# A decode block on one core: the last 5 KB of each row of one K tile loaded by transfers of 112, 3, 3, 3, 3, 2, 1 and 1 rows

## The chip, the core and the metric

The kernel runs on one core of one Trainium2 chip. The metric is the device time of one execution in microseconds (us); the time before is the median of three runs, 354.95 us (354.88 to 355.61). The profile is of one further execution, which took 354.43 us.

## The reference, cut to what matters

One token passes through an attention block with a long cache and a small feed-forward block. There are 32 query heads and 8 groups of K and V ("kv heads"); each group has 32768 cached positions of 128 values in bf16, which is 8 MB of K and 8 MB of V.

```python
mod = (silu(c) @ w_mod)                      # sa, ca, ga, sb, cb, gb
h = layernorm(x) * (1 + ca) + sa
q = h @ wq                                   # 32 heads of 128
scores = einsum('bhqd,bhkd->bhqk', q, k) * Dh ** -0.5   # k: 8 groups, 32768 positions
p = softmax(scores)
o = einsum('bhqk,bhkd->bhqd', p, v)
x = x + ga * (o @ wo)
h = layernorm(x) * (1 + cb) + sb
x = x + gb * (relu(h @ w1) @ w2)
```

With one token there is little arithmetic for each byte: nearly all of the work is to bring 8 groups of K and V, and the weights, into the core's memory once.

## The kernel before

**Tiles.** K and V of one group are loaded as one tile each, `Ksb{g}` and `Vsb{g}`, of 128 partitions (rows) by 256 positions by 128 values: 64 KB in each row. In the code a tile counts as four steps `u` of 64 positions (`TK = 64`, `NTILE = 4`). All large tiles live in one pool, `ring`, with three buffers (line 77), so the tile that is loaded next must wait until the tile three places before it has been read to the end. `wmq_sb` (the weights of the modulation and of Q) is the first of them and `tail_sb` (the weights `wo`, `w1`, `w2`) the last.

**The stream.** The list `stream` (lines 148 to 155) names every large load in order: `k0` (first half), `w_mod`, `wq`, `k0` (second half), then `k(g+1)` and `v(g)` in turns, from group 5 on in halves, at the end `wo` in four pieces, `w1` in two and `w2` in six. `need(key)` (line 158) loads along this list until the key asked for is there. `load` (line 108) makes the tile and its source, and calls `stream_dma` (line 140), which issues one DMA from the SP queue and keeps the order of the list. All these loads thus stand in one queue, and SP issues each as soon as its buffer is free. Nothing else but the 1 KB output is issued from SP; the two loads of `c` and `x` (1 KB in 8 rows each, line 169) are issued from ACT.

**The work on a tile.** For K: `turn_k` (line 416) transposes an eighth of the tile with DVE, in place (line 426), and `scores` multiplies it on PE (line 445) into `S_ps`. Then `softmax` works with PE, DVE and ACT. For V: `pv` (line 499) multiplies the probabilities by V on PE (line 507), in a loop for groups 0 to 4. In the main loop (line 630) the scores of group g+1 are worked out ahead of `pv` of group g. A K buffer comes free when its scores are done, a V buffer when its `pv` is.

**Loading order around the change.** Group 3's K, `Ksb3`, goes into the buffer that `Vsb0` held. It comes behind `Ksb2` and `Vsb1` in the queue, and ahead of `Vsb2` and `Ksb4`. `turn_k(3, u, half)` reads positions 64u + 32·half to 64u + 32·half + 31 of each row.

**Counting landings.** Each DMA is given one of eight completion counters, in turn. An instruction that needs a tile waits for the counters of the DMAs that wrote it. A DMA whose counter was used by an earlier DMA that nobody has waited for yet makes SP wait for that earlier one first.

**The end.** After the last piece of `w2` has landed, 16 small matmuls (line 767), two operations of DVE (lines 772 and 774) and the 1 KB output follow.

Of the kernel before, what the change touches and what calls it, by code (L numbers as in the profile page):

```python
# [17 lines left out]
def kernel(  # L18
# [15 lines left out]
    P = 128  # L34
# [8 lines left out]
    TK = 64  # L43
    NTILE = Sk // (P * TK)
# [8 lines left out]
    W1P = [(0, KT - 1), (KT - 1, KT)]  # L53

    OUT0, OUT1 = 30, 34
    assert Dh == 128 and REP == 4 and D == 512 and FT == W2P[-1][1] and NTILE == 4
    scale = float(Dh) ** -0.5
    eps = 1e-5
# [8 lines left out]
    def wo_v(i):  # L67
        g0, n = WOP[i]
        return A_wo[g0 * REP * Dh:(g0 + n) * REP * Dh, :].rearrange("(p r) d -> p r d", p=P)
# [32 lines left out]
    def piece(name, at, n):  # L102

        if name not in pieces:
            pieces[name] = ring.tile([P, NTILE * TK * Dh], BF16, tag="slot", name=name)
        return pieces[name][:, at:at + n]

    def load(key):
        kind = key[0]
        if kind == "wm":  # L110
            t = piece("wmq_sb", 0, WM).rearrange("p (kt n) -> p kt n", kt=KT)
            src = wm_v
        elif kind == "wq":
            t = piece("wmq_sb", WM, WQ).rearrange("p (kt n) -> p kt n", kt=KT)
            src = wq_v
        elif kind in "kv":
            g, steps = key[1], key[2]
            src = (kv if kind == "k" else vv)[g, :, TK * steps[0]:TK * (steps[-1] + 1), :]
            name = f"Ksb{g}" if kind == "k" else f"Vsb{g}"
            t = piece(name, TK * Dh * steps[0], TK * Dh * len(steps)).rearrange("p (j d) -> p j d", d=Dh)  # L120
        elif kind == "wo":
            g0, n = WOP[key[1]]
            t = piece("tail_sb", g0 * REP * D, n * REP * D).rearrange("p (r d) -> p r d", d=D)
            src = wo_v(key[1])
        elif kind == "w1":
            k0, k1 = W1P[key[1]]
            t = piece("tail_sb", WO + k0 * Dff, (k1 - k0) * Dff).rearrange("p (kt f) -> p kt f", f=Dff)
            src = w1_v[:, k0:k1]
        else:
            f0, f1 = W2P[key[1]]  # L130
            t = piece("tail_sb", WO + KT * Dff + f0 * D, (f1 - f0) * D).rearrange("p (f d) -> p f d", d=D)
            src = w2_v[:, f0:f1]
        stream_dma(t, src)
        if kind in "kv":
            for i, u in enumerate(steps):
                loaded[(kind, g, u)] = t[:, TK * i:TK * (i + 1), :]
        else:
            loaded[key] = t

    def stream_dma(dst, src):  # L140
        i = nc.sync.dma_start(out=dst, in_=src)  # L141
        tc.stamp_issue_order_token(i.ins, "sp_stream")
        if last_loop:

            tc.add_manual_dep(i.ins, last_loop[0], mybir.DependencyInfo(
                mybir.DependencyClass.NoSync, mybir.DependencyReason.DATA))

    whole, halves = [(0, 1, 2, 3)], [(0, 1), (2, 3)]
# [9 lines left out]
    def need(key):  # L158
        while key not in loaded:
            load(stream[pos[0]])  # L160
            pos[0] += 1
        return loaded[key]
# [19 lines left out]
    for hp in range(4):  # L182
        h, par = hp // 2, hp % 2
        src = AP(ib.tensor, ib.offset + 64 * h + par, [[ib.ap[0][0], P], [0, 4], [2, 32]])
# [130 lines left out]
    for u in range(2):  # L315
        for half in range(2):
            t = need(("k", 0, u))[:, 32 * half:32 * half + 32, :].rearrange("p j d -> p (j d)").bitcast(F32)
# [488 lines left out]
```

## Time and profile before

| what | value |
|---|---|
| runs before | 354.88, 354.95, 355.61 us |
| profiled execution: its time, its span | 354.43 us, 352.5 us |
| DMA traffic | 149.58 MB, mean 424 GB/s over the span |
| issues of K and of V (8 MB tiles, and pieces of them) | 11 and 12 |
| PE busy, DVE busy | 276.4 us (78%), 200.9 us (57%) |
| a transposition of an eighth of K on DVE | 2275 ns, 64 of them |

The span runs from the first to the last instruction; 1.9 us of the profiled execution lie around it. There are 16 DMA engines, and each large transfer is cut into packets, one for each row: 128 packets, 8 on each engine, with one packet of 4 bytes on each engine behind them that counts the landing up. A transfer's data have landed when all the engines that carry it have counted. The trace keeps start, duration and size of every packet but not the number of its engine.

### The profile page before, as it was taken

What the parts mean: (1) busy time and instruction counts of PE and PEld (TensorE: products, weight loads), DVE (VectorE), ACT (ScalarE), POOL (GpSimd) and SP (SyncE); (2) the same over time, 40 slices, a digit from 0 to 9 for tenths busy, and PEclk for the clock granted to TensorE, in tenths of its full rate; (3) what the DMA queues carried; (4) which work ended last, traced back from release to release, by engine and by line L of the source; (5) the groups of instructions that cost most, each with busy time, mean ns of one, the idle gap of its engine ahead of it and who ended that gap; (6) DMA issues with size and microseconds to landing.
All of it is one profiled execution on the core that took longest, in us unless ns stands there. A gap on an engine that the chain in (4) does not pass through costs nothing. (4 is left out here: it accounts for less than half of the span.)

```text
span 352.5 us, 3650 instructions
## 1 busy us (share of the span) xinstructions
PE 276.4 (78%) x1285; PEld 112.7 (32%) x1285; DVE 200.9 (57%) x226; ACT 25.1 (7%) x69; POOL 3.1 (1%) x15
## 2 busy tenths in 40 slices
PE   0055891995998599976998499867999789989976
PEld 0021330341333233422433233322444334434433
DVE  6662464984079613974099506975684357744142
ACT  1200103002000200001000200011000100011000
POOL 2000000000000000000000000000000000000000
PEclk9996897698999969996999989996999999999986
DMA  8999989989999999899899899999999999999995
GB/s 353 404 436 440 496 372 469 461 379 469 431 409 455 424 424 461 387 448 469 387 454 469 387 455 461 396 402 450 435 422 424 450 429 420 433 454 403 429 413 217
DMA packets 5379, 149.58 MB, mean 424 GB/s; under 512 B 632, under 2 KB 888, under 8 KB 1784
## 3 DMA queue, kind: packets, MB, share of 16 engines
q1 hardware_dynamic: 5336, 149.43, 98.5%
q8 instruction: 8, 0.13, 0.1%
q14 instruction: 3, 0.02, 0.0%
q10 hardware_dynamic: 32, 0.00, 0.0%
HBM read 149.42 MB, written 0.00 MB: 424 GB/s over the span
## 5 line engine op out<-in xcount | busy, mean ns | idle before, releaser
L426 DVE STREAM_TRANSPOSE Ksb<-Ksb 128x2048 f32<-128x2048 f32 x60 | 133.1, 2275 | 59.6 <-DMA Ksb<-in_A_k_cache_dram 59.6
L507 PE MATMUL o_ps<-Vsb,P_g 128*16 (+1 forms) x512 | 126.6, 405 | 13.3 <-ACT P_g L482 10.0
L445 PE MATMUL S_ps<-Ksb,qbd 128*128 128x512 bf16 x512 | 120.8, 388 | 10.4 <-DVE Ksb L426 8.7
L445 PEld LDWEIGHTS <-qbd 128*128 128x128 bf16 x512 | 49.8, 99 | 77.7 <-issue 21.8
L507 PEld LDWEIGHTS o_ps<-Vsb,P_g 128*16 x352 | 33.6, 95 | 68.2 <-issue 38.3
L507 PEld LDWEIGHTS <-P_g 128*16 128x16 bf16 x160 | 13.8, 90 | 19.0 <-issue 0.4
L407 ACT COPY qbd<-qrep_sb 32x16 bf16<-32x16 bf16 x32 | 6.4, 201 | 175.2 <-PE S_ps L445 174.0
L487 DVE STREAM_TRANSPOSE P_g<-P_g 128x1024 bf16<-128x1024 bf16 x8 | 10.0, 1245 | 14.1 <-ACT P_g L482 14.1
L458 DVE TENSOR_REDUCE m_p<-S_ps 128x1 f32<-128x1024 f32 x7 | 8.6, 1223 | 12.7 <-PE S_ps L445 12.7
L309 PE MATMUL mod_ps<-wmq_sb,siluT 128*1 128x512 bf16 x24 | 3.6, 623 | 9.9 <-DMA wmq_sb<-in_w_mod_dram 9.9
L318 DVE STREAM_TRANSPOSE Ksb<-Ksb 128x2048 f32<-128x2048 f32 x4 | 8.9, 2280 | 1.7 <-DMA Ksb<-in_A_k_cache_dram 1.7
L463 PE MATMUL mT_ps<-ident_f,m_p 128*1 128x128 f32 x8 | 2.2, 270 | 8.9 <-DVE m_p L458 7.9
L482 ACT ACTIVATE P_g<-S_ps,nbias 128x1024 bf16<-128x1024 f32 x8 | 8.9, 1114 | 0.2
L493 PE MATMUL L_ps<-Lexp,ones_f 128*128 128x4 f32 x16 | 3.1, 263 | 6.4 <-DVE Lexp L490 4.3
L496 DVE RECIPROCAL Linv<-L_ps 128x4 f32<-128x4 f32 x8 | 1.3, 164 | 11.7 <-PE L_ps L493 11.7
L479 ACT ACTIVATE nbias<-Mb_ps 128x1 f32<-128x1 f32 x8 | 1.4, 171 | 88.1 <-PE Mb_ps L477 88.1
L542 PE MATMUL acc_ps<-mask_sb,Y 16*128 16x4 f32 x16 | 3.1, 258 | 5.5 <-DVE Y L538 5.5
L239 PE MATMUL xc_ps<-cx_sel,wmq_sb 16*128 16x2 bf16 x4 | 0.3, 172 | 8.8 <-DVE wmq_sb L233 8.8
L535 DVE TENSOR_TENSOR o_ps<-o_ps,smask 16x512 f32<-16x512 f32 x8 | 5.3, 668 | 2.8 <-PE o_ps L507 2.8
L573 DVE CAST o_sb<-o_ps 128x4 bf16<-128x4 f32 (+2 forms) x4 | 0.7, 166 | 9.9 <-PE o_ps L569 9.9
L493 PEld LDWEIGHTS L_ps<-Lexp,ones_f 128*128 128x128 f32 x16 | 2.6, 203 | 9.7 <-issue 6.4
L538 DVE TENSOR_REDUCE Y<-o_ps 16x128 f32<-16x512 f32 x8 | 5.4, 679 | 0.3
(116 smaller groups left out, 80.6 us busy)
## 6 DMA issues: line engine op xcount, KB each, us to landing
Ksb<-in_A_k_cache_dram SPq DMA_DIRECT2D x6, 4096.0 KB, 30.3
Vsb<-in_A_v_cache_dram SPq DMA_DIRECT2D x5, 4096.0 KB, 29.5
wmq_sb<-in_A_wq_dram SPq DMA_DIRECT2D x1, 4096.0 KB, 28.1
Vsb<-in_A_v_cache_dram SPq DMA_DIRECT2D x2, 2048.0 KB, 35.5
wmq_sb<-in_w_mod_dram SPq DMA_DIRECT2D x1, 3072.0 KB, 18.9
tail_sb<-in_A_wo_dram SPq DMA_DIRECT2D x1, 2048.0 KB, 22.7
tail_sb<-in_B_w_dram SPq DMA_DIRECT2D x1, 1344.0 KB
tail_sb<-in_A_wo_dram SPq DMA_DIRECT2D x1, 1024.0 KB, 24.8
```

The source lines that it names most:

```text
L309: nc.tensor.matmul(dst[j // 4][32 * (j % 4):32 * (j % 4) + 1, :], lhsT=src_T[:, kt:kt + 1], rhs=w[:, kt, j * 512:(j + 1) * 512], start=(kt ...
L318: nc.vector.transpose(out=t, in_=t)
L407: nc.scalar.copy(out=o, in_=i)
L426: t = nc.vector.transpose(out=KTt.bitcast(F32), in_=KTt.bitcast(F32))
L445: nc.tensor.matmul(S_ps_tiles[g], lhsT=qbd[g % 2][:, hp, 4 * (7 - s):4 * (7 - s) + P], rhs=KTv[:, 16 * sl:16 * sl + 16, h, :, par], start= ...
L458: behind_loop(nc.vector.reduce_max(out=m_p[:], in_=S_g.rearrange("p g f -> p (g f)"), axis=AX.X))
L482: nc.scalar.activation(out=P_g[:], in_=S_g.rearrange("p g f -> p (g f)"), func=ACT.Exp, bias=nbias[:], scale=scale, accum_out=l_g[:],)
L487: behind_loop(nc.vector.transpose(out=P_g[:], in_=P_g[:]))
L493: nc.tensor.matmul(L_ps[:], lhsT=ones_f[:], rhs=Lexp[:], start=True, stop=True)
L507: nc.tensor.matmul(o_tiles[g][:], lhsT=PT, rhs=Vx, start=False, stop=False, skip_group_check=True)
L535: nc.vector.tensor_tensor(out=o, in0=o, in1=smask[:].unsqueeze(2).to_broadcast([16, 4, Dh]), op=ALU.mult,)
L538: nc.vector.tensor_reduce(out=Y[:], in_=o.rearrange("p s d -> p d s"), op=ALU.add, axis=AX.X)
```

## The change

Only the load of `Ksb3` is different. Its 256 positions are cut at position `EDGE` = 4·64 − 20 = 236. The first 236 positions of all 128 rows come by one transfer (59 KB in each row). The last 20 positions (5120 B in each row) come by eight: rows 0 to 111 by one, and rows 112 to 127 by seven of 3, 3, 3, 3, 2, 1 and 1 rows. The order in the queue is: the 112 rows, the first 3 rows, the 128 rows of 59 KB, then the other six. The bytes in all, and what is computed, are as before.

```diff
+    UNEVEN, FEW = 3, [(112, 115), (115, 118), (118, 121), (121, 124), (124, 126), (126, 127), (127, 128)]
+    EDGE = NTILE * TK - 20
...
-        stream_dma(t, src)
+        if key[:2] == ("k", UNEVEN):
+            whole = slice(0, EDGE)
+            last = [(slice(a, b), slice(EDGE, None)) for a, b in [(0, FEW[0][0])] + FEW]
+            for part in last[0:2] + [(slice(0, P), whole)] + last[2:]:
+                stream_dma(t[part], src[part])
+        else:
+            stream_dma(t, src)
```

The order of the instructions shows these waits on SP's queue, beside those of before: the transfer of 2 rows waits for `Ksb2` to have landed, the first of 1 row for `Vsb1`, the second for the 112 rows of `Ksb3`; the load of `Vsb2` waits for the first 3 rows of `Ksb3`, and the load of `Ksb4` for the 128 rows of 59 KB. The load of `Vsb3`, which waited for `Ksb3`'s one transfer, waits for all nine.

## The prediction

> **What bounds the kernel now.** I read the end first (the chain of waits in order of time), then the DMA row of the page, then SP's timeline around the changed load.
>
> ```profile
> 313.07 0.33 SPq L141
> ...
> 313.44 24.82 DMA tail_sb<-in_A_wo_dram
> 338.25 0.02 issue
> 338.27 10.57 DMA tail_sb<-in_B_w_dram
> 348.84 0.04 issue
> 348.88 0.62 PE end_ps L767 x12
> ```
>
> Columns: start, length, what. The last 35 us before the end are transfers; from the last landing at 348.84 only 3.7 us remain to the span's end (352.5). What moves that landing moves the time.
>
> ```profile
> DMA  8999989989999999899899899999999999999995
> DMA packets 5379, 149.58 MB, mean 424 GB/s; under 512 B 632, under 2 KB 888, under 8 KB 1784
> q1 hardware_dynamic: 5336, 149.43, 98.5%
> q8 instruction: 8, 0.13, 0.1%
> ```
>
> Row DMA has the busy share of 40 slices in tenths: 8 or 9 in all but the last. The stretches around the changed load say the same:
>
> ```profile
> core 0: us, PE busy (x) PEld busy (x) DVE busy (x) ACT busy (x) POOL busy (x), PEclk, DMA share, GB/s
> 97.00:117.00 20.00, 18.07 (x80) 7.19 (x78) 17.73 (x9) 0.00 (x0) 0.00 (x0) 1.00 1.00 430
> 117.00:137.00 20.00, 15.59 (x60) 6.07 (x59) 5.10 (x10) 2.18 (x7) 0.00 (x0) 0.83 0.98 423
> ```
>
> So the 16 DMA engines are the bound, all the way. I went on into the packet records. Strung together (a packet starts within 4 ns of the end of the one before, and all engines run the same sequence of sizes), the big queue's packets fall into 16 chains without gaps, but for eight fetches of 16 KB of instructions ("q8"). Seven of these come before the last transfers are through, and each holds up one engine by 1.4 us (0.94 for itself, 0.47 more on the next packet), seven different ones. So the engines end the stream at different times: seven between 347.08 and 347.48, one at 347.92, eight between 348.62 and 348.84. The last eight set the end; the early ones have 1.4 to 1.8 us to spare.
>
> **What the change does, part by part.**
>
> *Packets.* A 65,536 B packet takes 2418 ns, one of 32,768 B 1213: 0.0368 ns per byte (27.2 GB/s) and 8 ns fixed, 4 of them overlapped. A 5120 B packet is then 196 ns, 193 from start to start. How many engines carry a transfer is in the counting packets: the page's 632 packets under 512 B hold 596 of 4 bytes on the big queue, 16 for each of 37 transfers of 128 rows and 4 for the 4-row output; the 8-row loads of `c` and `x` have 8 each. So 112 rows go over 16 engines, 7 each, and 3, 2 and 1 rows over as many engines; if each starts at the same first engine, that one gets 7 single rows, the next 5, the third 4. For every engine: 8 rows shortened by 188 ns (−1.51 us), 7 short rows and a second counting packet (+1.36): −0.15 us. The three get 7, 5 and 4 times 199 ns on top (193 and a counting packet of 6): +1.24, +0.85, +0.65 net.
>
> [...]
>
> *Rows that are out of place.* In every large transfer of this trace 16 engines move 128 rows in step, always in the same split. A block of 7 rows, and rows 112 to 127 through the first three engines, are written by other engines than those that otherwise fill these rows, while those are at full pace. The trace shows no such pair. Lower bound: 196 ns a packet as ever. Upper: two share one pace, so 392 ns a row, and the engine that is met loses as much. That is up to 14 x 0.196 = 2.7 us more on the engine with 7 + 7 rows and up to 11 x 0.196 = 2.2 us (7 own rows, 4 met) on one of those that own the last rows. No row tells the two apart, though an identical 27.2 GB/s on 16 engines, whatever the packet, looks like a limit that each meets on its own way. I take half the rows as met: +1.4 us on the fullest engine, +0.7 us (7 rows) on an ordinary one.
>
> [...]
>
> *SP and its waits.* Eight more issues at 0.33 to 0.53 us each are 3 to 4 us of SP. Cover, from SP's timeline:
>
> ```profile
> 102.11 0.33 SPq L141 DMA_DIRECT2D Ksb<-in_A_k_cache_dram  x1
> 118.46 0.33 SPq L141 DMA_DIRECT2D Vsb<-in_A_v_cache_dram  x1
> 140.68 0.33 SPq L141 DMA_DIRECT2D Ksb<-in_A_k_cache_dram  x1
> ```
>
> These are `Ksb3`, `Vsb2`, `Ksb4`. By the packets `Ksb2` landed at 98.0 (nothing to wait for), `Vsb1` lands at 117.4, `Ksb3`'s first packets are through some 2 us later. So the two single rows are issued at 117.5 to 120 and `Vsb2`, queued behind them on SP, at 120 to 121 in place of 118.46. Its first packet is due at 134.9: 14 us of cover, cost nothing. Without the cover each us is a us. `Ksb4` now waits for the 59 KB rows too, which land at 137 to 141 where it is issued at 140.68; its packets are due at 154. Nothing again.
>
> *DVE.* It waits for `Ksb3` in any case (the stretch before has 12.4 us of idle time for it). Tiles landing 1 to 3 us later eat into the 12.3 us that it idles before `Ksb4`. Nothing.
>
> *Sum.* The fullest engine is an early one or a late one with equal chance (of the eight engines that also carried `c` and `x`, the lowest eight if the order is fixed, four are early). Early: 1.24 + 1.4 − 1.6 = +1.0. Late: 1.24 + 1.4 − 0.1 = +2.5; ordinary late engines −0.15 + 0.7 = +0.55. Mean of the two: about +1.7. Against the profiled execution 354.43 + 1.7 = 356.1; the median of the runs lies 0.5 above it: 356.6.
>
> **The rivals.**
>
> (A) The first three engines are early ones and rows out of place cost nothing. Then the late engines gain 0.15 and the loaded ones stay within their 1.6: 354.8. For it: the sizes (+1.24 at most) fit the room. Against: by chance alone three of four early among eight is 1 in 14.
>
> (B) No cost of place, but one of the three is a late engine. Of 14 equal cases 7 have the fullest late (+1.0 to +1.24, since the late ones differ by 0.22), 4 the second but not the fullest (+0.6 to +0.85), 2 only the third (+0.4 to +0.65): weighted +0.9, 355.8. For it: four late among the eight. Against: nothing but the doubt on the cost of place.
>
> (C) The forecast: shared pace, +0.5 (ordinary engines alone) to +3.9 (all rows met, fullest engine late): about 356.6.
>
> (D) Faster by more than 0.7 us. Perfectly even engines would end at the mean of the 16 ends, 348.04, so 0.8 us is all there is, and 5 KB a row is too little for it; only if other fetches fall on other engines, as the program is a little longer. About 354.1.
>
> (E) SP's chain of waits runs later than I read it and `Vsb2` misses its place: each us behind 134.9 costs one. Against: 14 us of cover. If it happened, some +2 us, inside (C)'s bounds.
>
> **How the numbers follow.** C 0.48, B 0.22, A 0.22, D 0.05, E 0.03. Below 0.2% (0.7 us, about what a measurement of this kernel can tell from no change) fall A, a third of B and a twentieth of C: same 0.32; faster 0.06 (D, rounded up); slower 0.62. Time 356.6. The range goes from A's 354.7 up to 358.0 (most of C's upper part, with its +3.9 left out). The likeliest case alone: 355.5 to 358.5.
>
> **What would show it.** The 5120 B packets: 196 ns each says A or B, near 390 says C. `Ksb3`'s last landing, 136.8 now: up to 1.5 us later without shared pace, 2 to 4 with it. The last landing at 348.84 moves by as much as the time does, and `Vsb2`'s issue stays ahead of 134. I am wrong if the stretches of 20 us around `Ksb3` keep 423 GB/s or more and the last landing stays: then it was A. If DMA's share falls below 0.9 somewhere from 117 to 157, it was E.

## The result, and the profile after

The changed kernel took 357.98 us in the median (357.55 to 359.14, six runs) beside 354.94 us (354.5 to 355.61, six runs) for the kernel before: a ratio of 1.0089, with a 95% interval of 1.0067 to 1.0110. That is 3.0 us more, at the upper edge of the range and nearly twice the 1.65 us (356.6 beside 354.95) that were forecast. The profiled execution took 357.55 us, 3.1 more than that of before.

The end of the chain of waits after the change, in the columns of before (start, length, what):

```profile
315.93 0.33 SPq L150
...
316.30 24.74 DMA tail_sb<-in_A_wo_dram
341.04 0.02 issue
341.06 10.57 DMA tail_sb<-in_B_w_dram
351.63 0.04 issue
351.67 0.62 PE end_ps L776 x12
```

The pieces have the lengths of before to a tenth of a us, but the landing behind them has moved from 348.84 to 351.63: the 2.8 us were lost before the tail. The stretches of 20 us, DMA share and GB/s last, show where. Before, the third and the fourth were

```profile
137.00:157.00 20.00, 18.33 (x83) 7.52 (x80) 17.73 (x9) 0.00 (x0) 0.00 (x0) 1.00 0.98 424
157.00:177.00 20.00, 15.60 (x64) 6.24 (x63) 5.85 (x11) 2.18 (x7) 0.00 (x0) 0.83 1.06 459
```

and after the change the four are

```profile
97.00:117.00 20.00, 18.05 (x79) 7.21 (x78) 17.73 (x9) 0.00 (x0) 0.00 (x0) 1.00 0.93 393
117.00:137.00 20.00, 15.56 (x61) 6.10 (x60) 5.11 (x10) 2.18 (x7) 0.00 (x0) 0.83 1.06 417
137.00:157.00 20.00, 17.10 (x71) 6.91 (x69) 16.57 (x9) 0.00 (x0) 0.00 (x0) 0.91 0.99 417
157.00:177.00 20.00, 15.29 (x61) 5.98 (x59) 6.26 (x11) 2.18 (x7) 0.00 (x0) 0.83 1.00 433
```

The first three add up to 50 GB/s less than before, 1.0 MB in 20 us, which at 424 GB/s is 2.4 us; with the fourth it would be 3.6 us. This is rough: a stretch counts a packet where it starts, and one 64 KB packet on each of 16 engines is 1.0 MB. Yet the engines are not idle: the share stays at 0.93 or more, and packets simply last longer. The page says the same of the whole (424 GB/s before):

```profile
DMA packets 5540, 149.59 MB, mean 420 GB/s; under 512 B 664, under 2 KB 920, under 8 KB 1944
```

SP's queue did what the waits said, and nothing came of it:

```profile
102.17 20.05 SPq L150 DMA_DIRECT2D Ksb<-in_A_k_cache_dram  x9
122.32 0.35 SPq L150 DMA_DIRECT2D Vsb<-in_A_v_cache_dram  x1
140.46 0.35 SPq L150 DMA_DIRECT2D Ksb<-in_A_k_cache_dram  x1
```

The nine issues of `Ksb3` last until 122.22, `Vsb2` follows at 122.32 in place of 118.46, some 14 us ahead of its first packet (136.7), and `Ksb4` is issued at 140.46 in place of 140.68.

The packet records show the loss itself. There are three kinds of packets around the load:

| packets | usual length | after the change |
|---|---|---|
| 128 of 5120 B | 196 ns | first 35 at 196; mean 288, longest 485 |
| 128 of 60,416 B | 2229 ns | 18 above 2300, the longest 3675 |
| of 65,536 B next to them (end of `Vsb1`, start of `Vsb2`) | 2418 ns | 12 of `Vsb2`'s first at 3.2 to 3.7 us, a few at 2.5 to 3.5 |

The time above the usual length is 11.8, 17.8 and 13.7 us: 43 us on 16 engines, 2.7 us for each. Only a quarter of it stands in the short packets. When `Vsb2` began, just 13 short packets were still to come, in three chains, and 12 first packets of `Vsb2`, 11 of them in other chains, went 0.8 to 1.3 us over their length.

### The profile page after: what moved, and what is told of

Its sections match the earlier page's. It is cut to its first block, busy times and chain, and to the rows that moved or that the text cites. A ratio compares the mean times of both kernels' runs of the same rounds, so it can differ in the third digit from the quotient of the medians.

```text
span 355.8 us, 3665 instructions
## 1 busy us (share of the span) xinstructions
PE 277.7 (78%) x1285; PEld 112.7 (32%) x1285; DVE 200.9 (56%) x226; ACT 25.1 (7%) x69; POOL 3.1 (1%) x15
```

## The experiments

The theories at the start: P, a row that is written by another engine than its usual one shares a pace with that one; H, the sources (all engines read the same stretch of rows 64 KB apart); N, short packets and further transfers as such; and a surplus on three engines. Times are set beside the runs of the kernel before on the same chip (354.88 us for the first four, 355.01 us for the others). "Excess" is the sum over the packets around the load above their usual length, divided by 16. It is what an engine lost on average in the profiled execution; the time follows the engine that ends last, so it can grow by more.

**The cut alone.** All rows by 128-row transfers:

```diff
+            rest = slice(EDGE, None)
+            for part in [(slice(0, P), rest), (slice(0, P), whole)]:
+                stream_dma(t[part], src[part])
```

> Ksb3 comes by two transfers of 128 rows each: the last 5120 B of the rows, then the first 59 KB. Every engine moves the same bytes as before, each row through the engine that always moves it; only the cut at 5 KB is left of the change. Theory P (a row written by another engine than its usual one shares a pace with the usual one): 5120 B packets of 196 ns, time +0.05 us against before, 354.95 to 355.0. Theory H (the sources: all engines read the same last 5 KB of rows that lie 64 KB apart): 5120 B packets of 300 ns and more, and +1 us or more. Theory N (short packets and further transfers by themselves): +0.5 us or more.

Measured: 355.41 us, ratio 1.0012 (1.0000 to 1.0024). All 128 packets of 59 KB took 2229 ns, and the short ones 196 in the median; excess 0.03 us. The 0.5 us by which the median is higher is at the limit of what these runs tell apart. In its profiled execution 0.5 us was lost ahead of the load already: `Ksb2`'s counting packets, in the mean of 16, ended at 97.5 in place of 97.0. So neither the cut nor 5 KB packets from places 64 KB apart cost what the change costs. That speaks against N, as far as it rests on short packets, and against H.

**Even load, rows out of place.** The same with 112 and 16 rows:

```diff
+            rest = slice(EDGE, None)
+            for part in [(slice(0, 112), rest), (slice(112, P), rest), (slice(0, P), whole)]:
+                stream_dma(t[part], src[part])
```

> The last 5120 B of the rows come by a transfer of 112 rows (7 on each engine) and one of 16 rows (1 on each engine), then the 59 KB by 128 rows. Every engine has its 8 rows as before, but 7 + 1 of them are rows of other engines. Theory P, by a model of shared pace laid over the packet times of before: +1.1 to +1.8 us, packets of 5120 B at 250 to 350 ns in the mean. If the cost of the change is that three engines carry more than their share: +0.05 us. Theories H and N: as the two transfers of 128 rows.

Measured: 357.63 us, ratio 1.0073 (1.0053 to 1.0094), +2.75 us, above what the model gave. Short packets 307 ns in the mean; 16 of the 59 KB packets over 2300 ns. Excess 2.1 us. No engine carries more than its eight rows here, and the interval overlaps that of the change: most of the cost comes without a surplus on three engines.

**Another source.** The nine transfers of the change, with the short ones reading one unbroken stretch:

```diff
+            rest = slice(EDGE, None)
+            flat = src[0:P // 2].rearrange("p j d -> (p j) d")
+            flat = flat[0:P * 20].rearrange("(p j) d -> p j d", p=P)
...
+                stream_dma(t[r, rest], flat[r])
```

> The nine transfers of the change with the same rows, the same order and the same bytes in each, but the eight short ones read their 5120 B rows from one unbroken stretch of K in place of places 64 KB apart (the last 20 positions of Ksb3 are then other rows of K than the reference's). Theory P: as the change, +2 to +3.5 us, 5120 B packets of 300 ns and more. Theory H: the packets fall back to about 200 ns, and what is left is the three engines' surplus, within their room: at most +0.5 us.

Measured: 358.28 us, ratio 1.0098 (1.0080 to 1.0117); short packets 284 ns in the mean, excess 2.8 us. The distance of the sources of the short rows does not matter; H is out for the change. Of the causes named, the side on which the rows are written and the number of transfers are left.

**Sixteen neighbours at a time.**

```diff
+            rest = slice(EDGE, None)
+            last = [(slice(16 * i, 16 * i + 16), rest) for i in range(8)]
+            for part in last[0:2] + [(slice(0, P), whole)] + last[2:]:
+                stream_dma(t[part], src[part])
```

> The last 5120 B come by eight transfers of 16 neighbouring rows (rows 0 to 15, 16 to 31, and so on; one row on each engine), two ahead of the 59 KB and six behind. Every engine carries 8 rows as before, one each time, but 16 engines write 16 neighbouring rows. [...] Surplus on three engines as the cause: +0.1 us. Theory N: more than with the two transfers of 128 rows, below 1 us.

Measured: 358.43 us, ratio 1.0101 (1.0084 to 1.0119), +3.55 us, more than the surplus (+0.1) or N (below 1) would cost. The short packets were at 325 ns in the mean; of the excess of 2.9 us, two thirds again stood in the long packets behind. As no engine has a surplus here, this run too does without one.

**Sixteen rows, every fourth.**

```diff
+            rest = slice(EDGE, None)
+            last = [(slice(a, a + 61, 4), rest) for a in (0, 1, 2, 3, 64, 65, 66, 67)]
```

> The last 5120 B come by eight transfers of 16 rows as in the run with 16 neighbouring rows, in the same order, but each takes every fourth row of one half of the tile (0, 4, .. 60; 1, 5, .. 61; .. 67, 71, .. 127). Sizes, counts and engines are the same; only which rows are written at one time differs. [...] If it only matters that a transfer has 16 rows, or that there are eight of them: +3.6 again.

Measured: 357.56 us, ratio 1.0069 (1.0052 to 1.0086), +2.55 us; short packets 258 ns, excess 1.7 us. The two runs have the same sizes, counts and waits. The times alone hardly tell them apart: their intervals touch, and they were measured on different chips. The packets do: the excess is 1.7 us in place of 2.9, and from `Ksb2`'s landing to `Vsb2`'s (means of their 16 counting packets) it takes 60.1 us in place of 61.2, where the kernel before takes 58.2. So it does matter which rows are written together. The sources differ as well (256 KB apart in place of 64 KB), but the run with one unbroken stretch showed no cost of that.

**Whole rows by 112 and 16.** No cut and no short packet:

```diff
+            for part in [slice(0, 112), slice(112, P)]:
+                stream_dma(t[part], src[part])
```

> Ksb3 comes whole rows at a time (64 KB each), by one transfer of 112 rows and one of 16; no column is cut and no packet is short. Each engine moves 7 + 1 rows as before, but rows of other engines. If the cost is the rows' place: +8 to +14 us (the model of shared pace; a third of the pace lost for as long as it lasts). If the cost hangs on short packets or the number of transfers: +0.1 us.

Measured: 376.91 us, ratio 1.0621 (1.0600 to 1.0642): +21.9 us, beyond every expectation, with the excess at 21.7 us. The page's GB/s in 40 slices and the stretches of 20 us:

```profile
GB/s 336 434 443 413 488 447 433 385 426 447 440 442 329 224 252 203 154 419 442 440 433 433 447 441 412 426 428 423 430 430 432 440 427 430 432 440 411 430 417 193
...
DMA packets 5395, 149.58 MB, mean 399 GB/s; under 512 B 648, under 2 KB 904, under 8 KB 1800
```

```profile
117.00:137.00 20.00, 15.59 (x61) 6.05 (x59) 5.11 (x10) 2.18 (x7) 0.00 (x0) 0.83 1.01 252
137.00:157.00 20.00, 3.93 (x19) 1.61 (x17) 0.00 (x0) 0.00 (x0) 0.00 (x0) 0.65 0.95 161
157.00:177.00 20.00, 14.52 (x56) 5.88 (x57) 17.15 (x9) 0.00 (x0) 0.00 (x0) 0.75 0.97 417
```

Each engine carries 7 of the 112 rows. From 118.7 to 126.7 all 32 packets that started took 4.59 to 4.81 us in place of 2.42, half the pace. It did not stay so throughout: the 112 packets took 4.34 us in the mean, the shortest 2.76, 11 of them under 3 us, and none the usual 2.42. Then come the 16 neighbouring rows, one on each engine, with the first rows of `Vsb2` behind them: each of the 16 took 7.8 to 9.1 us, towards a quarter of the pace. The DMA share stays at 0.95 or more all the while: a packet that is held up counts as busy for as long as it lasts. The sources of these 64 KB rows were not varied.

**Half and double the cut.** The change with 10 and with 40 positions cut off; the edit for 10 (for 40 it has 40 in the same place):

```diff
-    EDGE = NTILE * TK - 20
+    EDGE = NTILE * TK - 10
```

> The change with the cut at 10 positions in place of 20: the same nine transfers, with rows of 2560 B in the eight short ones. In the change the first three or so short packets of each engine keep their 196 ns, so some 15 to 20 KB for each engine seem to be taken up before the pace falls. If so, 7 rows of 2560 B nearly fit, and the time is +0.2 to +0.9 us. If the cost goes with the bytes: +1.5 us. If it goes with the number of packets and transfers: +3 us.

> The change with the cut at 40 positions: the same nine transfers, rows of 10,240 B in the eight short ones. Taken up first and then paid: +6.5 to +9 us. With the bytes: +6 us. With the number of packets: +3 us. The surplus of the fullest engine is then +2.5 us, past its room of 1.6 at most, and adds up to 0.9.

Measured: 356.25 us, ratio 1.0037 (1.0023 to 1.0051), and 362.03 us, ratio 1.0199 (1.0182 to 1.0216): +1.24 and +7.02 us, with the change's +3.04 between them. The number of transfers and packets is the same in all three, so N, which would cost the same in all, is out; the cost grows with the bytes, a little faster than they do (0.50, 0.61 and 0.70 us for each KB of the cut). In the packets it grows as they do: the excess is 1.2, 2.7 and 5.0 us, about 0.5 us for each KB. What the double cut costs beyond that lies at the end of the stream: three chains of packets, as many as carry the single rows, run on alone from 354.2 and stop at 354.6, 355.2 and 356.1. The page's last slice has 104 GB/s there, and 190 after the change. So the surplus on three engines does show, once it is large enough. With half the cut most short packets kept their 102 ns (mean 120) and the cost was there all the same: 17.3 of 19.5 us of excess lay in the packets behind. So the short packets that keep their length at the start (35 in the change, about two for each engine) are no free allowance, as had been supposed: the cost appears in those behind. The 7.02 us of the double cut do lie where an allowance was to put them (6.5 to 9), but the excess, which goes with the bytes, speaks against one.

## Why the prediction was right and wrong

**What bounds the kernel: right.** DMA set the end before and after, and the landing at 348.84 moved by 2.8 us while the time of the profiled executions moved by 3.1. It is the landing of the last piece of `w2` but one; the last piece's follows at 349.50, after the change at 352.27, and moved by as much.

**The packets: right where rows stay in place.** With the cut alone the packets were as long as the sum of fixed costs said (a short one 196 ns, a 59 KB one 2229). The counts of engines held as well: after the change 664 packets are under 512 B in place of 632, 16 more for the 112 rows and 16 for the seven transfers of 3, 3, 3, 3, 2, 1 and 1 rows.

**SP, the waits, `Ksb4`, DVE: right.** `Vsb2` was issued 1.3 us later than reckoned and still 14 us early. The rival with a late `Vsb2` is out. DVE began on `Ksb3` at 140.43 in place of 137.54, 2.9 us later, inside the 2 to 4 us that were given as the sign of a shared pace.

**Rows out of place: that they cost was right, the size and who pays were wrong.** This is the step that failed: "I take half the rows as met: +1.4 us on the fullest engine, +0.7 us (7 rows) on an ordinary one." In place of 0.7 us an engine lost 2.7 us in the mean of 16. The short packets, given as the sign (196 ns or near 390), lay between, at 288 in the mean. Two things were wrong in the step.

First, the share of rows that are met. With whole rows all 112 packets took longer than usual, 1.8 times their length in the mean, not half of them. Had only half the rows been met, part of the packets should have kept 2.42 us. None did. For 7 short rows at half pace an ordinary engine pays 7 x 0.196 = 1.4 us, not 0.7.

Second, who pays. The sum charged the engine that writes and the one that is met, and short packets alone. In the change 12 long packets of `Vsb2` were 0.8 to 1.3 us late, 11 of them in other chains than the 13 short rows that were left, and three quarters of the 43 us lay in long packets. The mean loss of 2.7 us is more than the 2.2 us that had been the upper bound for an engine that is met. So the bound itself was too low: it counted rows that meet, but rows in their usual split lasted longer with the others (those 12 of `Vsb2` 3.2 to 3.7 us where 2.42 is usual). Nor does it take a fullest engine, as the sum had it: without one, the runs with 112 and 16 rows and with eight times 16 rows cost 2.75 and 3.55 us. That 3.0 us still lie inside the bounds of the shared pace (+0.5 to +3.9) is partly luck, as their upper end was worked out for a fullest engine that is late.

Why rows in their usual split last longer too, and why the first short packets keep their length and the long ones behind pay, is not shown: no run took one pair of engines by itself. What was seen is how far it went: with whole rows all packets that started within 8 us went at half pace (4.59 to 4.81 us where 2.42 is usual), and the 16 neighbours behind them towards a quarter of the pace (7.8 to 9.1 us). Nor does a run show that a row has a usual engine, on which the step rests: the trace does not name the engines, and that 128 rows always go to them in the same way was the author's assumption. What the runs show in its place is that the last 5 KB of the rows had an excess of 0.03 us by one transfer of 128 rows and of 2.1 us by 112 and 16, with eight rows on each engine in both.

**The surplus on three engines** was worked out at +1.24 us for the fullest. The run with 112 and 16 rows, without a surplus, cost 2.75 us and the change 3.04, with intervals that overlap, so it decided little here; with double the cut it shows at the end. Whether the three were early or late engines in the change stays open: the trace does not name engines, and the chains cannot be told apart once a fetch has fallen between. The rivals A and B, which rest on that, are out for another reason: both had no cost of place.

**Faster by more than 0.7 us** did not come; no version tried here was faster than the kernel before.

## What to carry to other kernels

In this kernel, whose stream keeps all 16 DMA engines full, a transfer of 128 rows is more than a convenient size: cutting a single 8 MB tile into 112 rows and 16 cost 6% of the time (ratio 1.0621), though every engine moved the same bytes. Before bytes are moved from late engines to early ones, ask which rows will be written at the same time, not only how many bytes each engine gets; here cutting columns was nearly free (ratio 1.0012), and cutting rows as well was not (1.0073 by 112 and 16). And look for the loss in the packets behind the suspect ones and in GB/s, since the busy share does not fall (0.95 with whole rows by 112 and 16, at 161 GB/s).

## What the runs showed that was not expected

All 16 engines slowed together (4.59 to 4.81 us for 64 KB where 2.42 is usual, for 8 us) when a tile came by 112 rows, 7 on each. Short packets that cause the trouble can keep their usual length (102 ns, mean 120, with half the cut) while the packets behind them pay 17.3 of 19.5 us. And DMA's busy share stayed at 0.95 to 1.01 in the stretches in which the rate fell to 252 and 161 GB/s.
